# Rows gathered and stored mirrored in three of four blocks, one filter segment by DMA transpose, and the loads of the opening in another order

## The chip, the cores and the metric

One core of one Trainium2 chip. The metric is the device time of one launch in microseconds (us); smaller is better. Engines are named as the profile names them: PE is TensorE (PEld its weight loads), DVE is VectorE, ACT is ScalarE, POOL is GpSimd, SP is the engine whose queue (SPq) issues most DMAs. All arrays are bf16 and accumulate in f32.

## The reference

A long convolution with a gate, then a SwiGLU feed-forward network (FFN), with S = 2048 rows, D = 640 columns and F = 1728:

```python
def _A_ref(q, k, v, shift_k, ssm_k, ssm_D):
    k_shift = sum over t < 4 of k_pad[:, t:t+S, :] * shift_k[:, 3 - t]     # short causal filter
    kv = k_shift * v
    y = causal convolution of kv with ssm_k along S (by FFT of length 2 S) # one filter per column
    y = y + kv * ssm_D
    return q * y

x = A_q
h = x + _A_ref(_layernorm(x), A_k, A_v, A_shift_k, A_ssm_k, A_ssm_D)
h2 = h + (silu(_layernorm(h) @ w_gate) * (_layernorm(h) @ w_up)) @ w_down
```

(The two lines of `_A_ref` with words in them are a summary; the rest is cut to what matters.)

## The kernel before

Both sequences are cut into four blocks (the filter: segments) of 512 rows. The convolution is done block against segment in a basis of cosines and sines, applied by matmul: segments are transformed with WG, blocks with WX, the products are VectorE operations on 128 x 2560 tiles ("pairs", ten of them), and WI takes the sum back (`inverse`). The FFN of block n - 1 is put among the products of block n, so that TensorE has matmuls while VectorE multiplies. The program is a list of some 1,000 operations; `SEQUENCE` fixes the order in which they are emitted, and each engine executes its own in that order. Switches above it choose how a thing is done:

```python
RES = (0, 1, 2)
XACT = [(n, 1) for n in (1, 2, 3)]   # first normalisation of these blocks scaled on ScalarE
HOW = 'JJJJ'                         # J: the mirrored half of a block is flipped by TensorE; G: its rows are gathered mirrored
TRANS = {2: 28, 3: 28}               # segments transposed by DMA, the others by TensorE
```

(The comments are added here.) The inverse yields the even and odd parts es and os of a half block; es + os belongs to the rows in order, es - os to the mirrored rows. In mode J a matmul with the flip matrix turns it round, in mode G nothing is turned, since the rows of x were fetched in mirrored order and the result is stored in that order:

```python
if half == 0 or HOW[n] != "J":
    add("DVE", ..., TA or TS(y[:, 1 - half, :], es[m][:], os_[m][:]))
    if HOW[n] == "J":
        add("DVE", ..., TM(y[:, 1 - half, :], y[:, 1 - half, :], xln[:, 1 - half, :]))
else:                                                    # mode J, mirrored half: 4 matmuls of 320 columns
    for h in range(2):
        for part in range(2):
            nc.tensor.matmul(ps(g)[:, h, 0:NH], flip[part], (es, os_)[part][m][:, h * NH:(h + 1) * NH], ...)
    add("DVE", ..., TM(r3(y[:, 1 - half, :]), ps(g)[:, :, 0:NH], r3(xln[:, 1 - half, :])))
...
if HOW[n] == "G":                                        # load_x
    load(queue, x[:, 2:4, :], ...)                       # two tiles in order
    for q in (1, 0):                                     # two tiles gathered by GpSimd, by a table of row numbers
        nc.gpsimd.indirect_dma_start(out=x[:, q, :], in_=xq[:, :], in_offset=mirror(n, q), ...)
...
if "G" in HOW:
    load("SP", idx[:], idx_h.ap(), ["idx"], -94.5, 4)    # the table: 128 x 8 int32, 4 KB
```

(Cuts are marked by dots, and the calls are shortened.) `port` is a dummy `tensor_reduce` on VectorE, put beside a GpSimd instruction that must not meet a VectorE operation with two SBUF inputs. Times of some milestones are used all through, by these names: "V" the first flip of v on TensorE, "G0" the first segment transform, "products" the first pair, "hinge" the last inverse transform, "FFN 3" the FFN of the last block.

## Time and profile before

| | before |
|---|---|
| time, median of 3 runs | 289.55 us (289.06 to 289.61) |
| time, mean of 22 runs, those beside the first two sets of experiments | 289.27 us |
| span of the profiled execution | 287.11 us |
| k1 / V / G0 | 8.70 / 10.44 / 21.90 us |
| products / hinge | 33.90 / 217.65 us |
| FFN 3 / last matmul starts | 238.57 / 283.20 us |

The prediction below shows the lines of the page, of the rows in time and of the stretches that this table is read from. Two of its rows are worth a second look beforehand: the stretch from the products to the hinge, where PE and DVE are both busy for 99% of the time, and the hinge itself, which waits for the last VectorE product. I call that stretch the dense stretch.

One measure is my own and is used throughout. Between the starts of two successive matmuls an N-column matmul takes N/2.4 + 2.5 ns where nothing holds it up (the prediction reads 0.137 us for 320 columns and 0.216 us for 512 from the trace); what a gap is longer than that I call TensorE's lost time. VectorE's gaps are the length of a stretch less VectorE's busy time in it.

### The profile page before, as it was taken

How to read it: one execution, taken by the hardware profiler on the slowest of the kernel's cores; microseconds unless marked ns; L12 is line 12 of the kernel's file. 1: busy time of each engine (PE TensorE's matmuls, PEld its weight loads, DVE VectorE, ACT ScalarE, POOL GpSimd, SP SyncE). 2: the span in 40 equal slices, each digit the busy share in tenths (PEclk: the TensorE clock that was granted, in tenths of full speed). 3: DMA queues.
4: the chain of work that ended last, by engine and by line, in shares of the span. 5: the costliest groups of instructions: out<-in, count | busy, mean ns of one | idle time of the engine just before them, and what ended most of it. 6: DMA issues, size and time to landing. Idle time of an engine off the chain costs nothing.

```text
span 287.1 us, 4448 instructions
## 1 busy us (share of the span) xinstructions
PE 277.1 (97%) x1680; PEld 164.3 (57%) x1680; DVE 220.8 (77%) x299; ACT 198.4 (69%) x388; POOL 18.6 (6%) x22
## 2 busy tenths in 40 slices
PE   7899999999999999999999999999999989999994
PEld 2577777776444546764455467645455665444673
DVE  1738999999999999999999999999997511111222
ACT  5898755878785999367879995498958954545300
POOL 0003000010001001300004011000100110000000
PEclk9999999999999999999999999999999999999999
DMA  7999691363369847685653567456441391665011
GB/s 222 327 289 257 171 354 32 116 183 71 87 172 313 232 169 199 141 221 173 161 138 69 177 191 184 116 160 159 99 109 46 32 200 24 159 158 143 1 48 46
DMA packets 67946, 44.13 MB, mean 154 GB/s; under 512 B 25490, under 2 KB 66003, under 8 KB 67796
## 3 DMA queue, kind: packets, MB, share of 16 engines
q1 hardware_dynamic: 67778, 43.64, 56.0%
q8 instruction: 13, 0.21, 0.3%
q10 hardware_dynamic: 146, 0.20, 0.3%
q14 instruction: 9, 0.07, 0.1%
HBM read 37.28 MB, written 2.62 MB: 139 GB/s over the span
## 4 chain that ended last, share of the span: by engine, by line
DVE 54%; PE 22%; ACT 10%; DMA 7%; issue 5%; SPq 0%; DVEq 0%; ACTq 0%
DVE s L444 19%; DVE T L444 13%; PE psF L686 10%; PE psF L717 8%; DVE k L362 5%; DVE tT L700 3%; DMA hT<-in_A_v_dram 3%; PE psA L394 2%; DMA wu<-in_B_w_up_dram 2%; DMA k<-in_A_k_dram 2%; DVE k L367 2%; ACT sg L691 2%; ACT xln L561 2%; ACT junk L531 2%; ACT uc L698 2%
## 5 line engine op out<-in xcount | busy, mean ns | idle before, releaser
L686 PE MATMUL psF<-hT,wg 128*128 128x512 bf16 x280 | 68.6, 379 | 0.7 <-ACT uc L698 0.7
L686 PE MATMUL psF<-hT,wu 128*128 128x512 bf16 x260 | 63.6, 379 | 0.2 <-DMA wu<-in_B_w_up_dram 0.2
L717 PE MATMUL psF<-wd,tT 128*128 128x320 bf16 x448 | 63.3, 299 | 0.0
L717 PEld LDWEIGHTS <-tT 128*128 128x128 bf16 x448 | 43.8, 98 | 17.2
L444 DVE TENSOR_TENSOR s<-s,T 128x2560 bf16<-128x2560 bf16 x32 | 47.4, 1493 | 0.1
L444 DVE TENSOR_TENSOR T<-s,s 128x2560 bf16<-128x2560 bf16 x32 | 47.3, 1491 | 0.0
L691 ACT ACTIVATE sg<-psF 128x512 bf16<-128x512 f32 (+1 forms) x56 | 33.2, 596 | 20.2 <-DVE tT L700 12.0
L700 DVE TENSOR_TENSOR tT<-sg,uc 128x512 bf16<-128x512 bf16 (+1 forms) x56 | 23.0, 424 | 30.7 <-ACT uc L698 30.4
L686 PEld LDWEIGHTS <-wg 128*128 128x128 bf16 x280 | 27.4, 98 | 31.1 <-issue 1.2
L686 PEld LDWEIGHTS <-wu 128*128 128x128 bf16 x260 | 25.3, 98 | 30.2 <-DMA wu<-in_B_w_up_dram 0.7
L698 ACT CAST uc<-psF 128x512 bf16<-128x512 f32 (+1 forms) x56 | 32.8, 586 | 10.3 <-PE psF L686 9.8
L551 POOL TENSOR_TENSOR rstd<-var,mhalf 128x2 f32<-128x2 f32 (+2 forms) x15 | 18.1, 1207 | 213.9 <-ACT var L532 181.2
L345 PEld LDWEIGHTS <-s 128*128 128x128 bf16 x256 | 25.0, 98 | 9.7
L347 ACT CAST s<-psF 128x640 bf16<-128x640 f32 x32 | 22.1, 696 | 11.2 <-PE psF L345 11.1
L345 PE MATMUL psF<-wd,s 128*128 128x320 bf16 x192 | 28.5, 299 | 0.0
L439 ACT CAST s<-psA 128x640 bf16<-128x640 f32 x29 | 19.5, 696 | 9.4 <-PE psA L434 9.4
L531 ACT ACTIVATE junk<-x,sm 128x640 uint8<-128x640 bf16 x28 | 23.2, 830 | 0.5
L434 PE MATMUL psA<-kv,WX 128*128 128x320 bf16 x128 | 21.0, 299 | 0.0
L444 DVE TENSOR_TENSOR s<-s,s 128x2560 bf16<-128x2560 bf16 x14 | 20.8, 1487 | 0.0
L528 ACT ACTIVATE junk<-x 128x640 uint8<-128x640 bf16 x28 | 20.7, 738 | 0.0
L598 PE MATMUL psA<-s,WI 128*128 128x320 bf16 x128 | 19.0, 299 | 0.3 <-DVE s L444 0.2
L362 DVE TENSOR_TENSOR k<-k,w 128x2560 bf16<-128x2560 bf16 x12 | 17.7, 1488 | 0.0
(72 smaller groups left out, 242.9 us busy)
## 6 DMA issues: line engine op xcount, KB each, us to landing
k<-in_A_k_dram SPq DMA_DIRECT2D x12, 640.0 KB, 5.5
wu<-in_B_w_up_dram SPq DMA_DIRECT2D x24, 320.0 KB, 3.8
wg<-in_B_w_gate_dram SPq DMA_DIRECT2D x24, 320.0 KB, 3.3
x<-in_A_q_dram SPq DMA_DIRECT2D x4, 640.0 KB, 7.4
out_dram<-o SPq DMA_DIRECT2D x16, 160.0 KB, 2.1
v<-in_A_v_dram SPq DMA_DIRECT2D x12, 160.0 KB, 3.2
wd<-in_B_w_down_dram SPq DMA_DIRECT2D x3, 640.0 KB, 6.4
tT<-in_A_ssm_k_dram SPq DMA_DIRECT2D x2, 640.0 KB, 7.8
```

What stands on the lines that cost most here:

```text
L345: nc.tensor.matmul(ps(g)[:, h, 0:NH], WG[:, kt, ct * P:(ct + 1) * P], gT[p][:, kt, h * NH:(h + 1) * NH], start=(kt == 0), stop=(kt == 3))
L347: add("ACT", act(D), lambda g=g, ct=ct: nc.scalar.copy(r3(G[p][ct // 4][:, ct % 4, :]), ps(g)[:, :, 0:NH]), r=[g], w=[Gk[p] + "cs"[ct // 4 ...
L362: add("DVE", dve(4 * D), lambda: nc.vector.tensor_mul(kd[:], kd[:], w4[:]), r=["w4"] + ks, w=[kn], pr=pr)
L434: nc.tensor.matmul(ps(g)[:, h, 0:NH], WX[:, kt, ct * P:(ct + 1) * P], kv[:, base + kt, h * NH:(h + 1) * NH], start=(kt == 0), stop=(kt == 1))
L444: add("DVE", dve(n * D), lambda: f(o, a, b), r=ks(ak) + ks(bk), w=ks(ok), after=["WG0", "WG1"] if ok[:2] == "s7" else [], pr=pr)
L528: add("ACT", 0.74, lambda: nc.scalar.activation(junks[j][:], src, ACT.Copy, scale=-1.0 / D, accum_out=s[:, 0:1]), r=[xk], w=[k + "a", f"ju ...
L531: nc.scalar.activation(junks[j][:], src, ACT.Square, bias=s[:, 0:1], accum_out=s[:, 1:2])
L686: i = nc.tensor.matmul(ps(gr)[:, which, :], w[:, kt, cc * P:(cc + 1) * P], hT[b][:, kt, :], start=(kt == 0), stop=(kt == 4))
L691: apart(gr, 0, nc.scalar.activation(sg[s][:z, :], ps(gr)[:z, 0, :], ACT.Silu))
L698: add("ACT", act(MB), lambda gr=gr, s=s, z=z, merged=merged: nc.scalar.copy(uc[s][:z, :], ps(gr)[64:128, 0, :] if merged else ps(gr)[:, 1, ...
L700: add("DVE", dve(MB), lambda c=c, s=s, z=z: TM(tT[:z, c * MB:(c + 1) * MB], sg[s][:z, :], uc[s][:z, :]), r=[f"sg{s}", f"uc{s}"], w=[f"tT{c ...
L717: nc.tensor.matmul(ps(gr)[:, h, 0:NH], tT[:, c * MB + m * P:c * MB + (m + 1) * P], wd[:, c, h * NH:(h + 1) * NH], start=(c == 0 and not re ...
```

## The change

Its intent: take work from TensorE (24 flips, one segment's transposes, a few one-row matmuls), move block 0's first normalisation to ScalarE, load less ahead of the first block, and finish the last tile in two halves. The heart of the diff; the new `SEQUENCE` is left out:

```diff
-XACT = [(n, 1) for n in (1, 2, 3)]
+XACT = [(0, 1), (1, 1), (2, 1), (3, 1)]
-HOW = 'JJJJ'
+HOW = 'GGGJ'
-TRANS = {2: 28, 3: 28}
+TRANS = {1: 0, 2: 0, 3: 0}
 SEQUENCE = ...                       # 1017 operations, now 1013, reordered throughout
@@ gload
-                    dd = p == 0 and kt == 0
-                    nc.tensor.matmul(..., kc[:, c, kt * P:(kt + 1) * P], ident, start=True, stop=not dd)
-                    if dd:
-                        nc.tensor.matmul(..., ident[0:1, :], drow[:, c * P:(c + 1) * P], start=False, stop=True)
+                    nc.tensor.matmul(..., kc[:, c, kt * P:(kt + 1) * P], ident, start=True, stop=True)
+        if p == 0:
+            add("DVE", dve(D), lambda: TA(gT[0][0:1, 0, :], gT[0][0:1, 0, :], drow), ...)
@@ down
+        def last_tile(gr, m, s):
+            for h in range(2):        # 14 matmuls, an addition and a store of 320 columns each
...
+            if (n, m) == (NB - 1, 3):
+                last_tile(gr, m, s)
+                continue
```

## The prediction

> **What bounds the kernel now.** I read the page first, then the issue order of the matmuls in time, the chain that ended last, the stretches by stage, the GpSimd instructions, and last the opening 30 us. The page:
>
> ```profile
> span 287.1 us, 4448 instructions
> PE 277.1 (97%) x1680; PEld 164.3 (57%) x1680; DVE 220.8 (77%) x299; ACT 198.4 (69%) x388; POOL 18.6 (6%) x22
> DVE 54%; PE 22%; ACT 10%; DMA 7%; issue 5%; SPq 0%; DVEq 0%; ACTq 0%
> ```
>
> TensorE is busy for 97% of the span, but the busy time of pipelined matmuls does not by itself say that they run back to back. The rows in time do:
>
> ```profile
> 1.25 2.31 PE L288 MATMUL psF<-hl 128*128 128x512 bf16 x5 [1.25 <-DVE hl L278]
> ...
> 10.44 1.25 PE L402 MATMUL psF<-hT,perm 128*128 128x320 bf16 x4 [1.05 <-DMA hT<-in_A_v_dram]
> 11.47 3.26 PE L394 MATMUL psA<-s,perm 128*128 128x320 bf16 x14
> ...
> 21.90 3.42 PE L345 MATMUL psF<-wd,s 128*128 128x320 bf16 x24
> ...
> 230.42 0.43 PE L714 MATMUL psF<-x,perm 128*128 128x320 bf16 x2 [1.04 <-ACT o L723]
> ...
> 268.12 15.38 PE L717 MATMUL psF<-wd,tT 128*128 128x320 bf16 x112
> ```
>
> The last row is 112 matmuls in 15.38 us, 0.137 us each; a 512-wide group of five steps by 1.08 us, 0.216 each. These steps hold from 21.9 us to the end, with few named gaps, so a removed 320-wide matmul is worth 0.136 us where TensorE sets the pace. In the opening it is otherwise: the 14 of L394 take 3.1 us to the next row, 0.22 each. The stretches show a second engine that is just as full:
>
> ```profile
> 10.40:21.90 11.50, 11.46 (x80) 7.71 (x81) 6.47 (x6) 10.12 (x23) 0.00 (x0) 1.00 1.06 288
> 33.90:217.60 183.70, 181.73 (x1090) 106.33 (x1088) 182.77 (x237) 139.81 (x278) 13.49 (x9) 1.00 0.57 159
> 217.60:238.60 21.00, 19.91 (x145) 14.12 (x146) 8.23 (x18) 15.26 (x33) 2.18 (x4) 1.00 0.54 94
> 238.60:283.60 45.00, 44.66 (x248) 23.97 (x246) 8.30 (x18) 17.14 (x29) 0.00 (x0) 1.00 0.33 88
> ```
>
> The columns are the stretch, its length, then busy time (and count) of PE, PEld, DVE, ACT, POOL. From 33.9 to 217.6 us both PE (181.73) and DVE (182.77 of 183.70) are full: the FFN of the block before fills TensorE while VectorE does the spectral products. After 217.6 VectorE is nearly free and TensorE works off what is left. The hinge is the last inverse transform:
>
> ```profile
> 217.65 2.02 PEld L598 LDWEIGHTS <-WI 128*128 128x128 bf16 x16 [0.63 <-DVE s L444]
> ```
>
> It waited for the last VectorE product. So the end is about (time at which VectorE finishes its chain) + 66 us of TensorE work + the last store. From the last matmul (283.54) the tail is 3.6 us: one 0.82 us eviction, then a store.
>
> **What the Trainium skill says.** "TensorE: Matmul & The Clock Gate", section "Wait — 56ns, not 53.3ns?": warm matmuls start every N/2.4 GHz plus about 2.5 ns, cold ones every N/1.2 GHz. For N=320 that is 136 ns and 267 ns. The trace agrees: 0.137 late, and the four L402 begin 1.03 us before the next row, 0.26 each, so the opening is cold. "SBUF — State Buffer", section "Who interferes with whom": a VectorE tensor_tensor with both inputs in SBUF contends with a GpSimd instruction that reads SBUF; one with at most one SBUF input does not, and tensor_reduce never does. The trace agrees: the power op below starts at 114.67 and ends at 117.51, just after the dummy reduce at 116.87; the same shape took 0.69 at 53.46.
>
> ```profile
> 53.46 0.69 POOL L551 TENSOR_TENSOR rstd<-var,mhalf 128x2 f32<-128x2 f32 x1 [27.56 <-DVE var L511]
> 114.67 2.84 POOL L551 TENSOR_TENSOR rstd<-var,mhalf 128x2 f32<-128x2 f32 x1 [3.74 <-ACT var L532]
> 116.87 0.24 DVE L538 TENSOR_REDUCE idle<-junk 128x1 f32<-128x96 uint8 x1
> ```
>
> "DMA: Bandwidth & Descriptors", section "Anatomy of one DMA — SWDGE (gpsimd) path": a DMA from GpSimd costs about 2.0 us fixed plus bytes/436 GB/s, so about 2.4 us for a 160 KB tile. This kernel issues none before, so no run yet shows it.
>
> **The change, part by part.**
> (a) Mirroring in blocks 0 to 2. Rows of the two mirrored tiles are gathered in reverse order and stored back in that order, so es-os needs no flip through TensorE. Removed: 8 matmuls of 320 columns per block, 24 in all, 24 x 0.136 = 3.3 us of TensorE (the 24 of L618 outside block 3 lie in the dense stretch). VectorE, by the step from row to row: before, per half block, y 0.40, product 0.40, PSUM product 0.73, two adds 0.80 = 2.33; after, two y ops 0.80, one double product 0.73, one double add 0.73 = 2.26 (0.73 is the step of the 1280-wide L367). Six halves: -0.4 us.
> (b) Six gathers and six stores now come from GpSimd, and each store has a dummy reduce: 6 x 0.16 = +1.0 us of VectorE (0.16 is the step of a reduce).
> (c) Block 0's first normalisation goes to ScalarE: -4 x 0.36 = -1.4 us of VectorE, +4 x 1.2 us of ScalarE (L560 0.30 and L561 0.92), which is free there; two more dummy copies cost +0.2.
> (d) Segment 1 by DMA transpose: 20 transposing matmuls and 4 evictions of 0.69 leave the opening; the five one-row matmuls for the skip weight become one VectorE add (+0.4). In the trace the ten around L317 take 15.66 to 17.52 and the last ten 0.55, of which the interleaved one-row ones are about half: the saving is 0.55 + 0.7 for one segment and 0.8 for the one-row ones, about 2.1 us, all between 10.4 and 21.9 us.
> (e) The basis for the segment transforms is now issued ahead of the first DMA transpose. Before, that transpose held the load queue from 6.27 to 14.17 us:
>
> ```profile
> 6.27 7.90 SPq L304 DMA_TRANSPOSE wd<-in_A_ssm_k_dram  x1
> 14.21 0.58 SPq L274 DMA_DIRECT2D s<-const_wg  x1
> ```
>  Less is read early (half of x, no second segment), but the mirrored half comes through gathers beside k and v and the index table comes first: I allow +1 us on v's landing (320 KB at some 290 GB/s).
> (f) The very last tile is finished in two halves: the second eviction has 320 columns, (0.82 -> about 0.45), and its store half the bytes: -0.4 to -0.5 us at the end, certain.
> The words "second norms on VectorE" change nothing that I find: both kernels have eight statistics and sixteen scalings of the second norm there.
>
> **Sums.** TensorE: opening -2.1 +1.0 = -1.1, (a) -3.3, (f) -0.5: -4.9 us if TensorE alone decides. VectorE: -0.4 +1.0 -1.4 +0.2 +0.4 = -0.2 of work; its chain also starts earlier by the opening's 1.1 to 2.5 us (fewer matmuls before the first block's values are complete), and (f) comes on top: -1.8 to -3.2 if VectorE alone decides. With both full, the later one decides at the hinge. VectorE has about 2.8 us of small idle pieces after 25 us, some of them waits for evictions behind TensorE, which a lighter TensorE gives back in part: I add -0.8. I choose -4.0 us, between the two sums, as the new order was made for the new loads: 289.55 - 4.0 = 285.5 us.
>
> **The rivals.**
> 1. VectorE decides alone, and TensorE's 3.3 us turn into idle time before the inverses. For it: the wait at 217.65, and DVE 182.77 of 183.70. Against it: idle pieces remain on both. It makes 287 us.
> 2. GpSimd turns into a new wait. A gather or store that must read its index table while VectorE runs one tensor_tensor after another waits like the power op did, 2 us or more; a late store holds an output buffer, then a PSUM buffer, then TensorE. For it: the 2.84 above, and ScalarE already waited 4.1 us for stores. Against it: every store has its reduce, and the gathers are issued early. It makes 288 to 290.
> 3. The opening gains more than I count: with the basis there early and fewer matmuls, the transforms start 4 us earlier (at 18) and VectorE's chain with them. For it: 11.5 us hold only some 8 us of warm matmuls. Against it: v's landing at 10.4 starts it all, and that gets no earlier. It makes 282 to 283.
> 4. Transfers collide in the opening (DMA share already 1.06 from 10.4 to 21.9): block 1's k lands later behind the early transpose and stalls VectorE. It makes 288.
>
> **Range and chances.** The middle is 285.5. Full TensorE gain with rival 3 reaches 282.5, rivals 1, 2 or 4 reach 288.3; I take 282.7 to 288.3. Faster by over 2% means under 283.8, which needs nearly all of TensorE's sum or a better opening: 0.24. Slower by over 2% needs a stall of over 5 us beyond all gains: 0.03. Within 2%: 0.73.
>
> **What would show each step.** (a) Eight flips left, all of block 3, and 0.136 us steps where they stood. (b) Gathers and stores on GpSimd; wrong if ScalarE's output copies or TensorE's residual matmuls wait longer for stores than 4.1 and 1.0 us. (d), (e) The first segment transform starts at 20 to 21 instead of 21.9 and v lands no later than 11.5; at 18 or 19 rival 3 holds. Hinge: the last inverse starts at 213.5 to 215 instead of 217.65; if TensorE shows new gaps ending in VectorE's products, rival 1 holds. (f) From last matmul to end 3.1 us instead of 3.6. The prediction is wrong altogether if the clock of TensorE is not granted fully, or if TensorE loses more than 3 us to new waits after 33.9.

## More of the kernel before

In the dense stretch of the kernel before the lost time was 3.63 us, and VectorE's gaps were 0.93 us. (A trace can lack a few matmul records; then lost time is not given.)

## The result, and the profile after

| | runs | median us | lowest to highest | ratio to before, 95% interval |
|---|---|---|---|---|
| after | 4 | 288.1 | 287.47 to 288.22 | 0.9957 (0.9933 to 0.9981) |
| before, beside it | 4 | 289.31 | 288.63 to 289.61 | |

A ratio is the mean time of one kernel's fast runs over the mean of the other's fast runs of the same rounds, so it is not quite the ratio of the medians. All these runs were fast, with a granted clock of 1.0. The change gains 0.4%, or 1.2 us; 4.0 us were predicted. The time lies inside the predicted range, but near its upper end, where the rivals are.

The page of the kernel after:

```profile
span 285.5 us, 4397 instructions
...
PE 272.8 (96%) x1631; PEld 159.8 (56%) x1631; DVE 220.8 (77%) x299; ACT 199.8 (70%) x392; POOL 43.4 (15%) x34
...
DVE 48%; PE 29%; ACT 14%; issue 4%; DMA 4%; SPq 0%; ACTq 0%; DVEq 0%
```

TensorE has 49 matmuls and 4.3 us of busy time fewer (277.1 before), VectorE exactly as much as before (220.8), GpSimd more than twice as much (43.4 against 18.6). So the work did leave TensorE. The rows in time:

```profile
10.48 1.49 DVE L383 TENSOR_TENSOR k<-x,w 128x2560 bf16<-128x2560 bf16 x1 [6.04 <-DMA x<-in_A_k_dram]
...
12.55 0.71 PE L401 MATMUL psF<-hT,perm 128*128 128x320 bf16 x2 [1.51 <-DMA hT<-in_A_v_dram]
...
22.02 3.42 PE L344 MATMUL psF<-wd,s 128*128 128x320 bf16 x24
...
217.19 2.55 PE L597 MATMUL psA<-s,WI 128*128 128x320 bf16 x16 [0.39 <-DVE s L443]
```

They answer to the rows of before at 10.44 (flips of v), 21.90 (G0) and 217.65 (hinge). The flips of v start 2.1 us later, G0 only 0.1 us later, and the hinge is still a wait for VectorE's last product. The first row is new in importance: VectorE now stood idle for 6.04 us until k of block 0 had landed. In the kernel before, the same operation waited for an eviction by ScalarE, and k was there:

```profile
8.70 1.49 DVE L384 TENSOR_TENSOR s<-x,w 128x2560 bf16<-128x2560 bf16 x1 [4.49 <-ACT wd L319]
```

The stretches of the kernel after (columns as in the prediction: length, then busy time and count of PE, PEld, DVE, ACT, POOL):

```profile
12.55:22.02 9.47, 9.30 (x55) 5.93 (x56) 6.40 (x7) 6.67 (x17) 0.00 (x0) 1.00 1.00 262
...
34.02:217.19 183.17, 179.67 (x1067) 103.72 (x1065) 182.18 (x231) 145.12 (x288) 31.74 (x16) 1.00 0.57 157
217.19:237.72 20.53, 19.94 (x144) 14.07 (x145) 8.40 (x20) 15.29 (x34) 4.38 (x6) 1.00 0.48 105
237.72:282.20 44.48, 44.48 (x249) 24.05 (x246) 8.92 (x18) 16.99 (x29) 0.00 (x0) 1.00 0.34 91
```

The dense stretch holds 24 matmuls fewer (1067; 1091 before between the products and the hinge) and is 183.17 us long, 0.58 less than before; VectorE's busy time in it fell by 0.6 (182.8 to 182.18). Put side by side, from the milestones of the two profiled executions:

| part | before | after | difference |
|---|---|---|---|
| start to V | 10.44 | 12.55 | +2.11 |
| V to G0 | 11.46 | 9.47 | -1.99 |
| G0 to products | 12.00 | 12.00 | 0.00 |
| products to hinge (dense stretch) | 183.75 | 183.17 | -0.58 |
| TensorE's lost time in it | 3.63 | 6.37 | +2.74 |
| VectorE's gaps in it | 0.93 | 0.99 | +0.06 |
| hinge to FFN 3 | 20.92 | 20.53 | -0.39 |
| FFN 3 to last matmul | 44.63 | 44.22 | -0.41 |
| last matmul starts to end | 3.91 | 3.54 | -0.37 |
| span | 287.11 | 285.48 | -1.63 |
| time less span, mean of 22 and 10 runs | 1.79 | 2.00 | +0.21 |

The two parts in which the large gain was expected hold almost none of it. The flips' 3.3 us became 2.74 us of additional lost time on TensorE, and the 2.0 us saved between V and G0 were used up by v landing 2.1 us later. GpSimd's stores cost little. These are the lines of the table of waits (engine and line, then us in total, times, longest) for the 4.1 us and 1.0 us that the prediction names, before and then after:

```profile
ACT o L723 <- DMA out_dram<-o: 4.1, 2, 2.1
...
PE psF L714 <- ACT o L723: 1.0, 1, 1.0
```
```profile
ACT o L745 <- DMA out_dram<-o,idx: 5.5, 2, 3.6
...
PE psF L733 <- ACT o L745: 1.3, 2, 0.8
```

### The profile page after: what moved, and what is told of

Read it like the earlier page. It is cut to its first block, busy times and chain, and to the rows that moved or that the text cites. A ratio compares the mean times of both kernels' runs of the same rounds, so it can differ in the third digit from the quotient of the medians.

```text
span 285.5 us, 4397 instructions
## 1 busy us (share of the span) xinstructions
PE 272.8 (96%) x1631; PEld 159.8 (56%) x1631; DVE 220.8 (77%) x299; ACT 199.8 (70%) x392; POOL 43.4 (15%) x34
## 4 chain that ended last, share of the span: by engine, by line
DVE 48%; PE 29%; ACT 14%; issue 4%; DMA 4%; SPq 0%; ACTq 0%; DVEq 0%
DVE s L443 18%; DVE T L443 12%; PE psF L685 10%; PE psF L736 7%; PE psF L344 5%; DVE tT L699 4%; ACT xln L560 3%; DVE k L361 3%; PE psA L393 3%; DMA x<-in_A_k_dram 3%; ACT sg L690 2%; ACT uc L697 2%; PE psA L433 2%; DVE hl L563 1%; PE psF L714 1%
## 5 line engine op out<-in xcount | busy, mean ns | idle before, releaser
L736 PE MATMUL psF<-wd,tT 128*128 128x320 bf16 x420 | 60.2, 299 | 0.0
L736 PEld LDWEIGHTS <-tT 128*128 128x128 bf16 x420 | 41.1, 98 | 16.1
L550 POOL TENSOR_TENSOR rstd<-var,mhalf 128x2 f32<-128x2 f32 (+2 forms) x15 | 21.8, 1452 | 177.6 <-ACT var L531 149.3
```

What stands on the lines that cost most here:

```text
L550: add("POOL", 0.8, lambda: nc.gpsimd.tensor_tensor(rstd[:, c0:c1], var[:, c0:c1], mhalf[:, 0:c1 - c0], op=ALU.pow), r=deps + gkey + ["mhal ...
L736: nc.tensor.matmul(ps(gr)[:, h, 0:NH], tT[:, c * MB + m * P:c * MB + (m + 1) * P], wd[:, c, h * NH:(h + 1) * NH], start=(c == 0 and not re ...
```

## The experiments

Eighteen kernels ran, in five calls; kernels of one call shared a chip and the runs of the kernel before. Where a profile is read, it is that of one execution; the time is that of all. Two reasons were open from the start: why the dense stretch did not follow TensorE (theory: VectorE decides; rival: some new wait), and why the opening gained nothing (theory: the landing of k and v; rivals: the cold start of TensorE, the gathers, ScalarE). No run varied the cold start.

### The dense stretch: work added to one engine or taken from it

**TensorE's 24 matmuls put back, to no purpose** (e2). Each of the 24 is a flip of 320 columns into a PSUM tile that the next matmul overwrites. They bring back the flips' work, ahead of gate groups of the FFN, but not VectorE's wait for a flip.

```diff
 w = (wg, wu)[which][wb]
+if n < 3 and c < 8 and not which:
+    nc.tensor.matmul(ps(gr)[:, 0, 0:NH], flip[0], hT[b][:, 0, 0:NH], start=True, stop=True)
 for kt in range(5):
```

> The changed kernel with 24 needless matmuls of 320 columns put back (one ahead of each of the first 8 gate groups of blocks 0 to 2, overwritten by the real group, result right). Theory A (VectorE alone decides from 34 to 217 us, TensorE has slack there): the end moves by 0 to 0.8 us. Rival (TensorE decides, or both): 24 x 0.136 = 3.3 us longer, or at least half of that.

**Eight VectorE operations of 0.40 us added** (e3): a product written twice.

```diff
-lambda: nc.vector.tensor_mul(kv[:, q, :], kd[:, 0, :], vb[:])
+lambda: [nc.vector.tensor_mul(kv[:, q, :], kd[:, 0, :], vb[:]) for _ in range(2 if n < 3 else 1)]
```

> The changed kernel with each kv product of blocks 1 and 2 done twice (8 more VectorE operations of 640 columns, a step of 0.40 us each, 3.2 us in all, result right). Theory A (VectorE alone decides): 2.6 to 3.2 us longer. Rival (TensorE decides): under 1 us.

**Two VectorE additions of 1.40 us left out** (e4; wrong, although the outputs stayed within the tolerance).

```diff
-vop(TA, As, As, Tb, Ask, Tbk, Ask, pr)
+vop((lambda *a: None) if (j, p) in ((1, 1), (1, 2)) else TA, As, As, Tb, Ask, Tbk, Ask, pr)
```

> The changed kernel without two of the VectorE additions of the spectral products (one of block 2, one of block 3, 1.40 us each; result wrong on purpose). Theory A (VectorE alone decides): 2.2 to 2.8 us shorter. Rival (TensorE decides, or both are full): under 1 us shorter.

**The same two additions left out of the kernel before** (b). The edit is the same.

> The kernel before with the same two additions of VectorE taken away as in the earlier run with less work on VectorE (2.8 us less, wrong on purpose). If VectorE decided the dense stretch already before the change, the stretch gets shorter by 1 to 1.5 us as in the changed kernel (183.75 to 182.5); if TensorE decided it before (3.6 us of lost starts only), it stays within 0.4 us.

**Both at once: the additions left out of the kernel after, and the 24 matmuls put back** (e8).

> The changed kernel with the two additions of VectorE taken away (as in the run with less work on VectorE: stretch 181.9) and the 24 flips' worth of TensorE work put back (as in the run with the needless matmuls: stretch 183.8). If the two engines decide together, each limiting where the other has slack, the 24 matmuls now cost more than the 0.6 us they cost beside the full VectorE: stretch 183.0 within 0.3, which is 1.1 for 3.3 us of work. If TensorE has slack of its own there, 182.2 to 182.5.

The dense stretch of each, in the order e2, e3, e4, b, e8, one fence for each kernel:

```profile
35.45:219.24 183.79, 181.61 (x1090) 106.27 (x1089) 182.17 (x231) 145.48 (x288) 32.96 (x16) 1.00 0.58 157
```
```profile
36.47:222.27 185.80, 178.94 (x1061) 103.14 (x1058) 184.90 (x238) 144.75 (x287) 27.88 (x16) 1.00 0.58 155
```
```profile
33.78:215.69 181.91, 179.21 (x1066) 104.00 (x1065) 179.53 (x229) 145.03 (x288) 26.24 (x16) 1.00 0.58 158
```
```profile
34.79:217.95 183.16, 180.91 (x1079) 106.41 (x1090) 180.49 (x235) 139.93 (x278) 13.03 (x9) 1.00 0.56 159
```
```profile
35.25:219.46 184.21, 180.98 (x1078) 106.27 (x1089) 179.87 (x229) 145.69 (x288) 29.66 (x16) 1.00 0.57 156
```

The first number after the window is the length, the fourth pair DVE's busy time. (In the last two, some matmul records are missing, which is why PE shows 1079 and 1078.)

| kernel | flips on TensorE | DVE busy in the stretch | length | VectorE's gaps | time (median), ratio to before |
|---|---|---|---|---|---|
| before | yes | 182.8 | 183.75 | 0.93 | 289.3, 1 |
| b: before, less VectorE | yes | 180.49 | 183.16 | 2.67 | 288.7, 0.998 (0.9963 to 0.9997) |
| e2: after, matmuls back | yes | 182.17 | 183.79 | 1.62 | 289.71, 1.0015 (0.9991 to 1.004) |
| e8: both | yes | 179.87 | 184.21 | 4.34 | 290.0, 1.0029 (1.0006 to 1.0051) |
| after | no | 182.18 | 183.17 | 0.99 | 288.1, 0.9957 |
| e3: after, more VectorE | no | 184.90 | 185.80 | 0.90 | 291.71, 1.0085 (1.0061 to 1.0109) |
| e4: after, less VectorE | no | 179.53 | 181.91 | 2.38 | 286.75, 0.9923 (0.9897 to 0.9949) |

Read the length column. Without the flips, VectorE's work passes into the length almost one for one when it grows (e3: 2.72 us more busy time, 2.63 us more length): the kernel after is bound by VectorE, whose gaps stay at 0.9 to 1.0 us. Putting TensorE's 24 matmuls back costs 0.62 us for 3.3 us of work: they run in time that TensorE was losing anyway (its lost time falls from 6.37 to 3.79 us). That settles the question against TensorE's sum for the dense stretch.

The hinge shows the same by which engine comes last there. In before, b, e3 and after the inverse starts 0.06 us behind the end of VectorE's last product, and TensorE had lost 0.30, 0.09, 0.55 and 0.55 us to that wait. In e2, e4 and e8 TensorE lost nothing there: the product had ended 0.33, 0.24 and 0.68 us earlier, and the inverse follows straight on TensorE's own matmuls. The row of e2, without a wait, against that of after above (217.19):

```profile
219.24 0.98 PE L597 MATMUL psA<-s,WI 128*128 128x320 bf16 x6
```

The whole time is a weaker witness. By the ratios to before, e2 is 1.7 us longer than after, e3 3.7 us longer and e4 1.0 us shorter, so that e2's expectation (0 to 0.8 us at the end) was not met by time. In the profiles, what e2 and e3 have beyond the stretch lies mostly in the opening, which the edit of e2 does not touch (products at 35.45 in e2 and 36.47 in e3, 34.02 in after), and behind the hinge (68.67 and 68.59 us, 68.29 in after). Why is not shown.

The four rows with the flips tell why the change could not gain more. With them the stretch is 183.2 to 184.2 us long whether VectorE has 182.8 us to do or 179.9. So TensorE has a floor of its own near 183 to 184 us there (some 180 us of matmuls and at least 3 us of local waits), and VectorE, with some 182.8 us of work, had a floor of 183.7 us. The two floors lay within about half a microsecond of each other: the kernel before was balanced. Taking 3.3 us from one side alone moves the stretch down to the other side's floor and no further.

Three expectations of the stretch failed in a way that should be kept. Less VectorE work in the kernel before gave 0.59 us, between what the two theories had said (1 to 1.5, or within 0.4): both engines bound it. And e8, expected at 183.0, came out at 184.21, longer than e2 with more work on VectorE. In e4, 2.65 us less busy time gave only 1.26 us, where 2.2 to 2.8 were expected. After the work is taken away, VectorE's gaps grow (2.38 us in e4, 4.34 in e8). Of the waits that the table of waits names for VectorE in the stretch, those for ScalarE's evictions of the FFN tiles are 1.2 of 1.8 us in b, 1.6 of 3.2 in e8 and 0.5 of 1.6 in e4. In a fixed order each engine limits the other by turns, and the longer of two sums is only a lower bound. Which local wait makes e8 0.42 us longer than e2, with less work on VectorE, was not settled.

### Mirroring undone

**Mode J in all blocks, the order of the rest carried over by rule**.

```diff
-HOW = 'GGGJ'
+HOW = 'JJJJ'
 SEQUENCE = ...        # the 24 flips and their products at the place of the double operations, then repaired until legal
```

> The changed kernel with the gathered mirroring undone in blocks 0 to 2 (flips through TensorE as before: 24 more matmuls of 320 columns, six gathers and six GpSimd stores fewer, six dummy reduces fewer), the order of the rest carried over as well as it goes. Theory A (VectorE decides in the dense stretch; the flips were in TensorE's slack): within 1 us of the changed kernel in the stretch from the first product to the last inverse. Rival (TensorE's work decides): 3.3 us longer there. As the order had to be mended by rule, and not by search, new local waits may lengthen it by some us; then it tells little, and the idle time of VectorE in the stretch (0.9 us in the changed kernel) will show that.

Correct, but 336.16 us, ratio 1.1606 (1.1577 to 1.1636); VectorE's gaps in the dense stretch were 48.6 us.

```profile
DVE y L620 <- PE psA L617: 21.7, 3, 9.4
...
PE psA L597 <- DVE s L443: 14.8, 4, 9.1
```

VectorE waits up to 9.4 us for the flips and TensorE up to 9.1 us for VectorE: the repaired order is a bad one. This run says nothing about the flips; it shows only that such a switch cannot be undone alone when the order was made for it. The needless matmuls of e2 were the better experiment. Its opening is untouched by this and is used below.

### The end of the kernel

**The last tile whole again** (e7).

```diff
-parts = [(0, 4), (4, 8), (8, 12), (12, 14)] if (n, m) != (NB - 1, 3) else []
+parts = [(0, 4), (4, 8), (8, 12), (12, 14)]
...                                  # and in SEQUENCE, 1010 comes behind 1008 and 1009
-if (n, m) == (NB - 1, 3):
+if False:
```

> The changed kernel with its last tile finished whole as before, not in two halves. Step (f) of the prediction: 0.4 to 0.5 us longer, all of it after the last matmul starts (tail 3.9 to 4.0 us instead of 3.5). Rival: the split gains nothing, since the second half's store costs the same fixed time and the eviction's saving is lost to the later order of the matmuls: within 0.15 us of the changed kernel.

The control was **the kernel after itself**:

> The changed kernel itself, unaltered, as the control of this batch on the same chip. Every theory: the ratio of the earlier run again, 0.9957 within 0.002. Dense stretch (first spectral product to last inverse) 183.2 us, TensorE's lost time in it 6.4 us, VectorE idle 0.9 us in it.

The control gave 288.06 us, ratio 0.9957 (0.994 to 0.9974), dense stretch 183.16 us: the first result repeats. The whole last tile gave 287.96 us, ratio 0.9966 (0.9944 to 0.9989); by time, nothing can be said. In the profile it can. The last eviction of the control, then of the kernel with the whole tile:

```profile
282.17 0.49 DVE L719 TENSOR_TENSOR o<-psF,x 128x320 bf16<-128x320 f32 x1 [1.41 <-PE psF L714]
```
```profile
280.87 0.82 DVE L747 TENSOR_TENSOR o<-psF,x 128x640 bf16<-128x640 f32 x1 [2.98 <-PE psF L736]
```

With the split, the eviction shrinks from 0.82 to 0.49 us. From the last matmul to the end it took 3.55 us in the control and 4.15 with the whole tile, and from the hinge to the end 68.31 and 69.01. In these two profiles, splitting the tile is worth 0.6 to 0.7 us, more than predicted; the means of the six runs differ by only 0.16 us. In the profiled execution the opening was 1.4 us shorter with the whole tile (products at 32.50, control 33.91), which hides the gain there; where the others spent it is not recorded. Over the runs of one kernel the time varies by 0.7 us (b) to 4.1 us (o3). Three profiles of the unaltered kernel differ by 0.3 us in the span, nearly all of it in the opening: its dense stretch took 183.17, 183.16 and 183.18 us.

### The opening: order of the loads

**First try: k and v first** (e1). The numbers are the load queue's part of the order: 207 a v tile of block 1, 20 the index table, 24 segment 0, 21 k, 22 v, 71 x, 23 WG, 34 WX. Besides, ScalarE's copy of the first flipped v comes ahead of its first pass over a gathered tile.

```diff
-207 20 24 21 22 71 23 ... 34
+21 24 22 20 71 23 ... 34 207
```

> The changed kernel with its first loads in another order: k and v of block 0 no longer stand behind v of block 1, the index table and the first segment (order k, segment 0, v, index table, half of x, basis), so the gathers also start later. Theory A (the opening sets when VectorE's chain starts, and that chain sets the end): k lands near 7 instead of 10.5 us, VectorE starts with the tap weights at about 7.8, the first segment transform starts at 20 instead of 22.0, and the whole program is 1.5 to 2.5 us shorter than the changed kernel (about 286). Rival (the opening is not on the path): the end moves by less than 0.4 us.

A miss: 292.58 us, ratio 1.0045 (0.9993 to 1.0096), three of six runs slow, the profiled one too (clock 0.993). The row that explains it, ScalarE's first pass over a gathered tile:

```profile
20.23 0.74 ACT L527 ACTIVATE junk<-x 128x640 uint8<-128x640 bf16 x1 [6.92 <-DMA x<-in_A_q_dram,idx]
```

The index table stood behind k, segment 0 and v, so that the gathers were issued at 9.9 us and later and their rows landed near 20. ScalarE takes its instructions in order, waited 6.92 us for them, and its second copy of v came at 25.0. The first product started at 39.43 us instead of 34. The three fast runs took 288.10, 292.17 and 291.34 us, so what the wait costs in time is not shown. I concluded that the load order had to keep the table early.

**Second try: k first, then the table** (e5). ScalarE does all eight passes over block 0 ahead of its copy of y1, and issues the load of the first product's weight ahead of the flip matrix.

```diff
-207 20 24 21 22 71 23 ... 34
+21 20 24 22 71 23 ... 34 207
```

> The changed kernel with only the opening's loads and passes reordered: k is first on the load queue, then the index table, so that the gathers are not late as in the first try; ScalarE issues the weight of the first product before the flip matrix and does all eight passes over the first block before its copy of y1. Theory A (the opening's saved matmuls were eaten by the later landing of k and v): VectorE starts near 7 instead of 10.5, the first segment transform at 20 instead of 22.0, and all later milestones move by the same 2 us: end 2 us (0.7%) under the changed kernel. Rival B (the opening is bound by something else, such as TensorE's cold clock or ScalarE's evictions): VectorE starts earlier but the first segment transform stays within 0.5 us of 22.0, end within 0.5 us of the changed kernel. Rival C (gathers late again): the y1 copy and the first product late, end later than the changed kernel.

288.69 us, ratio 0.9972 (0.995 to 0.9994). VectorE did start at 7.77 instead of 10.25 in the control, but the flips of v did not follow:

```profile
12.44 0.69 PE L401 MATMUL psF<-hT,perm 128*128 128x320 bf16 x2 [0.78 <-ACT wd L316]
```

They now wait for ScalarE's evictions of segment 0, which had moved back. G0 came at 21.54 (control 21.90) and then waited for a transposed segment, and the products at 34.61. Theory A as I had put it falls: an earlier k alone is not enough. But a comparison of the transfers of these kernels showed something else.

### The opening: the index table

What the DMA engines moved in the first 16 us, in 40 slices of 0.4 us (first line: mean busy share of the 16 engines in tenths; second: GB/s). Before, and after:

```profile
DMA  0000659999977999999999999999999998799999
GB/s 0 0 0 0 88 79 307 391 366 348 351 200 222 312 298 342 371 326 333 374 374 378 400 390 394 396 365 362 353 356 336 318 226 81 162 289 292 290 418 127
```
```profile
DMA  0000748976556958999999999999999899899999
GB/s 0 0 0 0 77 113 311 359 231 205 192 184 200 198 175 259 335 307 342 370 349 384 413 419 384 430 377 366 373 414 443 358 406 467 348 343 367 330 338 357
```

After, the rate is 175 to 231 GB/s from the ninth to the fifteenth slice (3.2 to 6.0 us), and the engines are busy for only 50 to 70% of the time in all of these but one; before, there is a dip of two slices. I call this the hole. k and v come behind it in the same queue. The difference that I saw in the queue was the index table, 4 KB in 128 packets of 32 bytes, ahead of segment 0. Three runs moved it.

**The table on ScalarE's queue, behind the flip matrix** (o1):

```diff
-load("SP", idx[:], idx_h.ap(), ["idx"], -94.5, 4)
+load("ACT", idx[:], idx_h.ap(), ["idx"], -94.5, 4)
```

> The changed kernel with the 4 KB index table loaded by ScalarE's queue, behind the flip matrix, instead of by the load queue ahead of segment 0. In five of six profiles with the table ahead of segment 0 the transfers fell to some 190 GB/s for about 3 us while segment 0 was read, in none of the four profiles without it there. Theory A (the table's 128 packets of 32 bytes hold the queues up): no such hole, the flips of v start at 11.0 instead of 12.6, the first segment transform at 20.5 instead of 22.0, spans 1.5 us shorter on average than the changed kernel's (287.87 us in time on average): 286.4. Rival B (the hole is chance, or comes from the order of the other loads): spans as the changed kernel's within 0.4 us on average, flips of v at 12 to 13.

**The table on GpSimd's queue** (o2; `"POOL"` in the same place):

> The same with the table loaded by GpSimd's own queue, at the same place in the order. Theory A: as the run before, unless the table lands so late there that the gathers are issued after 6 us and land after ScalarE wants them; then the first product is late, not the flips of v. Rival B: as the changed kernel within 0.4 us.

**As o1, and the v tile of block 1 moved from the first place of the load queue to behind WX** (o3):

```diff
-207 24 21 22 71 23 ... 34
+24 21 22 71 23 ... 34 207
```

> The table on ScalarE's queue, and besides a 160 KB tile of v that only block 1 needs moved from the first place of the load queue to behind the basis of the x transforms. Theory A and the queue's order: 160 KB at 300 GB/s are 0.5 us, so the flips of v start another 0.5 us earlier, at 10.5, and the spans are 0.4 to 0.5 us shorter than those of the run with the table alone: time 285.9. Rival: v is not what the opening waits for by then, and the spans stay.

o1: 286.76 us, ratio 0.9921 (0.9901 to 0.994). o2: 286.61 us, 0.9918 (0.9898 to 0.9939). o3: 287.36 us, 0.9957 (0.9917 to 0.9996), with one run of 290.51 among six; its flips of v came at 11.76, not at 10.5, so the order of that tile gained nothing, and its interval holds both outcomes. The transfers of o1:

```profile
DMA  0000926999999966999999999999999999899999
GB/s 0 0 0 0 134 38 243 392 378 340 320 271 259 270 197 228 317 375 381 394 394 397 387 407 385 421 427 397 443 375 406 352 380 396 298 365 319 358 340 331
```

The hole is gone, and the flips of v start at 11.12 (o1) and 10.99 (o2).

**The control and o1 again**, and, as the decisive test, **the kernel before with nothing added but the table's load ahead of the first segment that it loads, segment 1** (nobody reads it, and this kernel has no gathers):

```diff
-add(q, dur, lambda: eng.dma_start(out=dst, in_=src), ...)
+add(q, dur, lambda: ([nc.sync.dma_start(out=idx[:], in_=idx_h.ap())] if w == ["kch1"] else []) + [eng.dma_start(out=dst, in_=src)], ...)
```

> The changed kernel once more, unaltered, so that it shares chip and rounds with the next run. Ratio 0.9957 within 0.002; in the profile probably a stretch of some 3 us near 190 GB/s while segment 0 is read and the flips of v at 12 to 13 (5 of 6 profiles so far), else at 11.0.

> The changed kernel with the index table on ScalarE's queue, again. If the table's place is the cause: 1.0 us (0.35%) under the changed kernel of this call, ratio to before 0.992 within 0.002, no stretch near 190 GB/s, flips of v at 11.0 to 11.2. If the first result was luck of the chip: the same ratio as the changed kernel, 0.9957.

> The kernel before with nothing but a needless load of the index table put ahead of its first segment on the load queue (nothing reads it; no gathers). If the table alone makes the slow stretch: transfers near 190 GB/s for about 3 us, flips of v at 11.8 to 12.5 instead of 10.4, and 1 us longer on average (ratio 1.003 to 1.004). If the slow stretch needs the gathers or the other order of the loads too: flips of v within 0.4 us of 10.4, ratio 1.000.

The control gave 287.31 us, 0.9941 (0.9919 to 0.9963); o1 again 286.86 us, 0.9932 (0.9914 to 0.9949), flips of v at 10.67. These two alone would not be told apart by time. The kernel before with the table: 290.5 us, ratio 1.0045 (1.0026 to 1.0064), which is 1.3 us longer, and two views show why, the transfers and the flips of v in time:

```profile
DMA  0000558944365698999999999999999999995389
GB/s 0 0 0 0 144 115 315 297 115 100 136 197 192 244 278 307 311 345 362 364 364 394 384 397 394 390 366 364 358 354 362 337 346 307 230 160 82 43 197 288
```
```profile
12.07 1.25 PE L402 MATMUL psF<-hT,perm 128*128 128x320 bf16 x4 [0.79 <-DMA hT<-in_A_v_dram]
```

The hole is there, and the flips of v start at 12.07 instead of 10.44. So the table's load in this place is a cause by itself, without gathers and without the new order. No run put another small load there, or the same 4 KB in longer rows, so it is not shown that the tiny rows make the hole, and not any further load at this point. Over all profiles, the mean of the four slices from 3.2 to 4.8 us, worked out from this view:

| profiles | mean GB/s, 3.2 to 4.8 us | V |
|---|---|---|
| 9 with the table ahead of the first segment and k (after, its two controls, e2, e3, e4, e7, e8, and before with the table) | 137 to 237 in eight, 340 in one (e7) | 12.07 to 13.22; e7 11.02 |
| 11 others | 307 to 396 in all | 10.44 to 12.44 |

Of the eleven, only the three with another order of the loads, e1, e5 and o3, have V later than 11.2. In e5 the table does stand ahead of segment 0, but behind k, and there is no hole (381 GB/s); an expectation above counts it among those without the table there. In o1 and o5, whose table's packets run at 5 to 7 us, a dip of two or three slices lies at that time; but e6, which loads no table, has one too (217 GB/s at 5.6 us).

What happens inside the hole is open. The table's own packets are not long: the 128 of them start between 2.9 and 3.5 us and take 9 ns each by the trace. It is what follows them, the first segment in packets of 1024 bytes, that comes slowly, with engines idle for part of the time; a dip without a hole, as in e7, happens too. The Trainium skill, "DMA: Bandwidth & Descriptors", section "Why small descriptors are slow (HBM only)", speaks of a fixed cost for each small packet; 128 such costs do not make 3 us here, as the 9 ns show.

### What is left of the opening

Two profiles show the opening that the prediction had expected (G0 at 20 to 21): e6, which has the new order but neither table nor gathers, with G0 at 20.61, and e7, which has both but no hole, with 20.50. Moving the table did not reach it. In o1, V came 1.4 us earlier than in after, but G0 only 0.5 us earlier in the profile (21.37 against 21.90) and the spans 1.1 us shorter on average (284.77 in six runs; 285.87 in the ten of after and its first control). The rows of ScalarE in o1:

```profile
14.34 0.74 ACT L527 ACTIVATE junk<-x 128x640 uint8<-128x640 bf16 x1 [3.29 <-DMA x<-in_A_q_dram,idx]
...
16.41 0.67 ACT L403 CAST y<-psF 128x640 bf16<-128x640 f32 x1
```

With the table later (the gathers start at 7.53, after at 4.29), ScalarE waits for the gathered tile, and its copy of the flipped v comes behind that. **The copy ahead of the pass, with the table on ScalarE's queue and on GpSimd's** (o5, o6):

```diff
-... 61 74 53 75 51 62 54 6 ...     # 74: first pass over a gathered tile, 53 and 54: flip and copy of v
+... 61 53 54 74 75 51 62 6 ...
```

> The changed kernel with the index table on ScalarE's queue and, besides, ScalarE's copy of y0 ahead of its first pass over a gathered tile. With the table alone moved, that pass waited 3.3 us for the gathers (they land at 14.3), and y0 came at 16.4 behind it, so that the first segment transform started 10.3 us after the flips of v instead of 9.5. If that wait is what is left of the lost opening: the transform starts 9.5 us after the flips of v, at 20.5, and the kernel takes 286.1 us (ratio 0.9895 to 0.991). If not: as with the table alone, 286.9 (0.992).

> The same with the table on GpSimd's queue. Both theories: as the run before within 0.3 us.

o5: 286.37 us, ratio 0.9898 (0.9875 to 0.992). o6: 286.74 us, 0.9909 (0.9889 to 0.993). The copy moved to 11.93, but G0 only to 21.12 in o5 (21.59 in o6), not to 20.5: the expected mechanism was not the main one. What sets G0 is not settled. VectorE's opening chain starts when k lands, and TensorE's flips when v lands; in the kernel before, k had landed before VectorE was ready for it. G0 follows VectorE's start by 11.54 us in the profile of after (10.48 to 22.02), 11.56 in e7 and 11.67 in o5, but by 12.35 in the second control, 12.34 in o6 and 12.61 in e3; it follows V by 9.2 to 10.6 us in the profiles with the load order of after. And in e5 VectorE started 2.5 us earlier than in the control, and G0 came only 0.4 us earlier. Both engines wait for a landing (VectorE 6.04 us for k and TensorE 1.51 us for v in the profile of after), and neither alone explains G0.

Both beat the kernel before by 0.9 to 1.0%, and their medians are below those of the changed kernel, by 0.6 to 1.7 us. o5 is the fastest kernel; that it beats o1 is not shown, since their intervals overlap.

## Why the prediction was wrong

**The mechanism of the sums was right, the choice between them wrong.** The prediction had VectorE's work as -0.4 +1.0 -1.4 +0.2 = -0.6 us (the last term of its sum, +0.4, lies in the opening), and the dense stretch shrank by 0.58 us, VectorE's gaps nearly unchanged at 0.93 and 0.99. That the numbers meet so well is partly luck. Counted in the two traces, (a) is -0.65 us in this stretch. The reduces are +0.65, since only four of the six stand there. The normalisation is -0.71, since only two of its four scalings stood there before; the others were at 27.35 and 28.11 us. The dummy copies are about 0 (three before and three after), and one product kv that the new order puts ahead of the stretch is -0.39. The unaltered operations took 0.5 us more. The prediction had TensorE's saving (a) as 3.3 us; the 24 matmuls did leave the stretch, and 2.74 us came back as lost time. The step that failed is "I choose -4.0 us, between the two sums". Where two engines are both full, the later one decides, as the same paragraph says; a value between the sums had no ground. With 1.1 us for the opening and 0.5 for the end, -4.0 us leaves -2.4 for the dense stretch, where -0.58 was measured. Rival 1, "VectorE decides alone", held, and its 287 us was the better estimate.

**"I add -0.8" for small idle pieces given back by a lighter TensorE.** Measured: nothing (gaps 0.93 and 0.99). The 2.8 us of idle pieces after 25 us from which it was taken are a misreading, too: from 25.00 to 217.65 us VectorE was busy for 191.51 of 192.65 us, which leaves 1.14, and the table of waits names no wait of VectorE there.

**(d) was right:** 2.1 us predicted between v's landing and G0, 1.99 measured. This part varies from profile to profile, though: 11.46 to 12.42 us in the three profiles with the load order of before, 9.22 to 10.61 in those with the order of after.

**(e) was mis-sized, and its reason missed.** "I allow +1 us on v's landing" measured +2.11 in this profile. The text names the index table ("comes first") but allows only for the 320 KB of the gathers; the table's place cost 1.3 us when it was put alone into the kernel before. The prediction of G0 at 20 to 21 failed by 1 us, and with it the opening's net gain of 1.1 us: the products began 0.12 us later than before. The step also watched v alone. k landed late too, and VectorE waited 6.04 us for it.

**(f) was right in kind, under-sized:** -0.4 to -0.5 predicted, -0.6 to -0.7 measured in one profile against the whole tile.

**The new stores (rival 2) did not matter.** ScalarE's wait for stores went from 4.1 to 5.5 us and TensorE's behind it from 1.0 to 1.3, both over the limits that the prediction set for (b), but the part from the hinge to FFN 3 was 0.39 us shorter all the same. What the rival described did happen: one gather took GpSimd 6.43 us, beside VectorE's products. But the dense stretch has no wait for it. **Rival 4** named the opening's transfers, but as a later k of block 1 and a collision of volumes; the runs show the order of the queue, for k and v of block 0. **Rival 3**, an opening that gains more, is not what happened.

**Not foreseen:** TensorE lost 1.39 us between the hinge and FFN 3 before and 1.01 after, and behind it 0.45 and 0.04, together 0.8 us of gain that no step of the prediction has; and 0.2 us more outside the span, told at the end.

With the table moved (o5), the gain over before is 1.0%, or 2.8 us: within the prediction's own sum for "VectorE alone decides", -1.8 to -3.2, with most of the opening that it had expected (G0 at 21.12).

## What to carry to other kernels

When two engines are both over 98% busy in a stretch, add up the change for each and take the later one; what is taken from the other turns into its idle time, and the profile of before shows this only as a balance, not as slack. In an opening, ask what each load has ahead of it in its queue and watch all the tiles that the first engines wait for, not one; here a load of 4 KB ahead of a large one cost more than its bytes. Where the variation between executions sits in one part (here the opening), compare the other parts in the profile: the dense stretch repeated within 0.02 us. And look at a wait's last arrival: the hinge told in each run which engine decided.

## What the Trainium skill lacked or had wrong

- "DMA: Bandwidth & Descriptors", section "Anatomy of one DMA — SWDGE (gpsimd) path": by its 2.0 us plus bytes/436 GB/s, a 160 KB tile takes an estimated 2.4 us. In the profile of after, three gathers of that size took 3.0 to 3.7 us from issue to landing, the two of the opening 7.2 and 7.3, and one 8.3; stores with an index table took 3.5 to 5.2. The issuing instruction itself took 1.0 to 1.2 us on GpSimd in five of the six gathers and 6.43 us in the sixth (124.44 us), beside VectorE's products, which fits "SBUF — State Buffer", section "Who interferes with whom".
- No page tells that a 4 KB table of 32-byte rows ahead of a 640 KB load on the same queue holds the following transfers at 137 to 237 GB/s (mean from 3.2 to 4.8 us, eight of nine profiles), against 307 to 396 in eleven others, though its own packets take 9 ns each.
- No page tells that a kernel which issues DMAs from GpSimd has more time outside the profiled span: time less span was 1.98 to 2.14 us on average for each of the kernels with gathers, and 1.77 to 1.81 for the kernel before and the three others without gathers.
- "TensorE: Matmul & The Clock Gate", section "Wait — 56ns, not 53.3ns?": the warm step of N/2.4 + 2.5 ns held wherever TensorE ran without a wait behind the opening (112 matmuls of 320 columns in 15.38 us); nothing to mend.
